# Strided attention before a dense layer: transposes by DMA instead of TensorE from batch 2 on

## The chip, the cores and the metric

One core of a Trainium2 chip runs the whole program. The metric is the device time of one execution in microseconds (us). Besides the unprofiled runs there is one profiled execution, from which all views of the trace come; its span goes from the first to the last instruction, and its own time is a little longer.

## The reference

Attention with two kinds of masks over 8 batches, 8 heads, 576 positions and 64 values a head, then a dense layer pair with a squared ReLU on the 4608 tokens:

```python
stride = 32
scores = (1 / sqrt(D)) * q @ k.T                     # per batch and head
rel = pos[:, None] - pos[None, :]
mask_local   = (rel >= 0) & (rel < stride)           # heads 0 to 3
mask_strided = (rel >= 0) & (pos[None, :] % stride == pos[:, None] % stride)   # heads 4 to 7
attn = softmax(where(mask, scores, -1e9))
x = (attn @ v).transpose(0, 2, 1, 3).reshape(4608, 512)
out = maximum(x @ w_in, 0) ** 2 @ w_out              # 512 -> 2048 -> 512
```

Inputs and output are float32; the kernel computes with bf16 operands.

## The kernel before, in words

**Units.** A unit `u` is one batch `b` and one pair of heads `p`; `u = 4*b + p`. Pairs 0 and 1 are local, pairs 2 and 3 strided. A local unit is cut into 6 blocks of 96 queries, a strided one into 8 groups of 72 positions (all positions with the same remainder by 8, which holds 4 residues by 32; the mask keeps the right one).

**Steps of a unit**, each emitted as one piece of the stream of TensorE:

- `step_T(u, "q")`, `step_T(u, "k")`: TensorE transposes q or k by blocks into one PSUM bank (L175; 8 matmuls for a strided unit, 6 for a local one), then ACT copies q (L188) and DVE copies k (L190) to SBUF as `qT`, `kT` (`kTl` for local units).
- `step_S(u)`: scores of both heads, one on each half of the array's rows (L214), into four PSUM banks; exponentials on ACT (L220) and masks on DVE (L226) are emitted one to four ticks later. A tick is one group of four dense matmuls.
- `step_D(u, part)`: attention times values, with a column of ones for the row sums (L251; two parts for a local unit, three for a strided one), a reciprocal and a product on DVE (L262, L263), into `x_l` or `x_s`.
- `step_E(u)`: TensorE transposes x (L274), and ACT (first three batches) or DVE (later) copies it into `xt[p]` (L280 local, L282 strided), where tokens are columns.

The PSUM pool `ps_t` of these steps has five banks, which are handed out in turn.

**Dense layers.** Nine chunks `c` of 512 tokens. `mm1(c, ff)` is a group of four matmuls into `ph` (L294) with a ReLU on ACT (L297) and a square on DVE one tick later (L298). `mm2(c, i)` is a quarter of a row block (L309); after the last quarter ACT copies `y` (L313) and SP stores it (L315).

**Order.** The steps of batch 0 run first. The list `groups` then holds all dense groups: chunk 0 and 1 one layer after the other, first layer of chunk 2 alone, and from chunk 3 on one group of `mm1(c)` alternating with one of `mm2(c-1)`. `stream_steps` lists the attention steps of batches 1 to 7, with T two units ahead of D, and `due` spreads them evenly between the groups, so that batch `b` is done before the first group of chunk `b` (batch 1 and 2 by groups 32 and 56). Everything is written out by hand: each engine runs its instructions in this order.

**Loads.** `loads(b)` is called at a given group (`load_at`: batch 2 at group 8, batch `b+2` two groups after batch `b` is done). It puts q, k and v of the local units and v of the strided ones on SP's queue as float32, with casts on POOL (L95, L123, L124, L139), and q and k of the strided units as casting DMAs on POOL's queue (L104), one unit after another between the casts. SP runs its issues in order, stores of `y` among them.

Of the kernel before, what the change touches and what calls it, by code (L numbers as in the profile page):

```python
# [9 lines left out]
BF16 = mybir.dt.bfloat16  # L10
# [4 lines left out]
def kernel(  # L15
# [9 lines left out]
    nc = tc.nc  # L25
    B, H, S, D = q.shape
    d_model, d_ff = moe_w_in.shape
    T = B * S
# [3 lines left out]
    QL = 96  # L32
    NL = S // QL
    NJ = 8
    RH = STRIDE // NJ
    SP_ = RH * NA
# [3 lines left out]
    singles = ctx.enter_context(tc.tile_pool(name="singles", bufs=1))  # L40
    qk_st = ctx.enter_context(tc.tile_pool(name="qk_st", bufs=2))
    qk_in = ctx.enter_context(tc.tile_pool(name="qk_in", bufs=3))
    qkT = ctx.enter_context(tc.tile_pool(name="qkT", bufs=3))
    v_st = ctx.enter_context(tc.tile_pool(name="v_st", bufs=2))
    small = ctx.enter_context(tc.tile_pool(name="small", bufs=4))
    x_pool = ctx.enter_context(tc.tile_pool(name="x_pool", bufs=2))
    g_pool = ctx.enter_context(tc.tile_pool(name="g_pool", bufs=2))
    r_pool = ctx.enter_context(tc.tile_pool(name="r_pool", bufs=4))
    y_pool = ctx.enter_context(tc.tile_pool(name="y_pool", bufs=3))

    PS = bass.MemoryType.PSUM
    ps_h = ctx.enter_context(tc.tile_pool(name="ps_h", bufs=2, space=PS))
    ps_y = ctx.enter_context(tc.tile_pool(name="ps_y", bufs=1, space=PS))
    ps_t = ctx.enter_context(tc.tile_pool(name="ps_t", bufs=5, space=PS))

# [11 lines left out]
    xt = [singles.tile([128, T], BF16, name=f"xt{p}") for p in range(4)]  # L67
# [6 lines left out]
    units = [(b, p) for b in range(B) for p in range(H // 2)]  # L74
    st = {}

    def is_local(u):
        return units[u][1] < H // 4

    def load_qk_local(u, eng, gate=None):  # L80
        b, p = units[u]
        s = st.setdefault(u, {})
        for name, src in (("q", q), ("k", k)):
            t = qk_st.tile([QL, 2, 6 * D], FP32, name=f"{name}_st")
            if gate is not None and name == "q":
                nc.gpsimd.tensor_copy(t[0:1, 0, 0:1], gate)
            eng.dma_start(out=t, in_=src[b, 2 * p:2 * p + 2]
                          .rearrange("h (p j) d -> p h (j d)", j=6))
            s[name + "f"] = t
# [9 lines left out]
    def load_qk_str(u):  # L99
        b, p = units[u]  # L100
        s = st.setdefault(u, {})
        for name, src in (("q", q), ("k", k)):
            t = qk_in.tile([SP_, 2, NJ * D], BF16, name=f"{name}_s")
            nc.gpsimd.dma_start(out=t, in_=src[b, 2 * p:2 * p + 2]  # L104
                                .rearrange("h (p j) d -> p h (j d)", j=NJ))
            s[name] = t

    def v_slot(u):
        b, p = units[u]
        return (b * 2 + p % 2) % NV  # L110

    def load_v_local(u, eng):
        b, p = units[u]
        t = vl_sts[p]
        for hh in range(2):
            eng.dma_start(out=t[32:128, NL * hh:NL * (hh + 1), :],
                          in_=v[b, 2 * p + hh].rearrange("(t p) d -> p t d", p=QL))
        st.setdefault(u, {})["vf"] = t
# [10 lines left out]
    def load_v_str(u, eng):  # L129
        b, p = units[u]  # L130
        t = v_st.tile([SP_, 2, NJ * D], FP32, name="v_st")
        eng.dma_start(out=t, in_=v[b, 2 * p:2 * p + 2]
                      .rearrange("h (p j) d -> p h (j d)", j=NJ))
        st.setdefault(u, {})["vf"] = t

    def cast_v_str(u, copy=None):
        s = st[u]
        t = vss[v_slot(u)]
        (copy or nc.gpsimd.tensor_copy)(t[:, :, 0:D], s["vf"].rearrange("p h (j d) -> p (h j) d", d=D))  # L139
        s["v"] = t  # L140
# [12 lines left out]
    def later(n, fn, key=None):  # L153
        pending.append((clock[0] + n, key, fn))
# [41 lines left out]
    def step_S(u):  # L196
        s = st[u]
        qT, kT = s["qT"], s["kT"]
        local = is_local(u)
        w, n = (QL, NL) if local else (SP_, NJ)  # L200
        kn = 128 if local else SP_
        hn = n // 2
        e = es[u % 4]
        s["e"] = e
        banks = [[None, None], [None, None]]
        for half in range(2):
            for row in range(2):
                banks[row][half] = ps_t.tile([128, 512], FP32, name="pt")
            for i in range(hn):
                t = half * hn + i  # L210
                klo = w * t
                for row in range(2):
                    rows = slice(64 * row, 64 * row + 64)
                    nc.tensor.matmul(banks[row][half][0:kn, w * i:w * (i + 1)],  # L214
                                     kT[rows, klo:klo + kn], qT[rows, w * t:w * (t + 1)],
                                     start=True, stop=True)

        def expo(row, half):
            lo = S * row + S // 2 * half
            nc.scalar.activation(e[0:kn, lo:lo + S // 2], banks[row][half][0:kn, 0:S // 2],  # L220
                                 AF.Exp, scale=scale)

        def masks(row):
            x = e[0:kn, S * row:S * (row + 1)].rearrange("p (t c) -> p t c", c=w)
            m = mask_loc if local else mask_str
            nc.vector.tensor_tensor(x, x, m.to_broadcast([kn, n, w]), op=ALU.mult)  # L226

        expo(0, 0)
        later(1, lambda: expo(0, 1), u)
        later(2, lambda: (masks(0), expo(1, 0)), u)  # L230
        later(3, lambda: expo(1, 1), u)
        later(4, lambda: masks(1), u)
# [33 lines left out]
    def step_E(u):  # L266
        s = st[u]
        b, p = units[u]
        x = s["x"]
        local = is_local(u)  # L270
        n, w = (NL, QL) if local else (NJ, SP_)
        px = ps_t.tile([128, S], BF16, name="pt")
        for t in range(n):
            nc.tensor.transpose(px[:, w * t:w * (t + 1)],  # L274
                                x[:, 2 * t:2 * t + 2, :].rearrange("p h d -> p (h d)"),
                                ident[0:w, 0:w])
        dst = xt[p][:, b * S:(b + 1) * S]
        copy = nc.scalar.copy if u < 12 else nc.vector.tensor_copy
        if local:
            copy(dst, px)  # L280
        else:
            copy(dst.rearrange("c (p j) -> c p j", j=NJ),  # L282
                                  px.rearrange("c (j p) -> c p j", j=NJ))
        st.pop(u)
# [43 lines left out]
    def first_steps():  # L328
# [9 lines left out]
        n = len(order)  # L338
        return [(fn, 0 if i < n - 8 else 4) for i, fn in enumerate(order)]

    def stream_steps(lo, hi, base):
        order = [T_(lo, "q"), T_(lo, "k"), T_(lo + 1, "q"), S_(lo), T_(lo + 1, "k")]
        ends = {}
        for u in range(lo, hi + 1):
            if u < hi - 1:
                order.append(S_(u + 1))
            if u > lo:
                order.append(E_(u - 1))
                ends[u - 1] = base + len(order)
            if u < hi:  # L350
                order.append(D_(u, 0))
                if u + 2 < hi:
                    order.append(T_(u + 2, "q"))
                order.append(D_(u, 1))
                if u + 2 < hi:
                    order.append(T_(u + 2, "k"))
                if not is_local(u):
                    order.append(D_(u, 2))
        return order, ends
# [5 lines left out]
    def loads(b):  # L365
        u = 4 * b
        for i in range(2):
            load_qk_local(u + i, nc.sync, gate=gates.get(b) if i == 0 else None)
            load_v_local(u + i, nc.sync)
        load_v_str(u + 2, nc.sync)  # L370
        load_v_str(u + 3, nc.sync)
        w_out = load_w_out if b == 1 else (lambda i: None)
        load_qk_str(u + 2)
        w_out(0)
        cast_qk_local(u, pool2)
        cast_v_local(u)
        load_qk_str(u + 3)
        w_out(1)
        cast_qk_local(u + 1, pool2)
        cast_v_local(u + 1)  # L380
        w_out(2)
        cast_v_str(u + 2)
        cast_v_str(u + 3)
        w_out(3)
# [92 lines left out]
    done_prev, g_prev = 0, 0  # L477
    ready = {1: 32, 2: 56}
    load_at = {8: 2}
    for b in range(1, B):  # L480
        g_end, s_end = ready.get(b, starts[b]), ends[4 * b + 3]
        if b == 1:
            g_prev = 9
        for g in range(g_prev, g_end + 1):
            due[g] = done_prev + (s_end - done_prev) * (g - g_prev) // (g_end - g_prev)
        done_prev, g_prev = s_end, g_end
        if b + 2 < B:
            load_at[g_end + 2] = b + 2
    done = 0
    for n, g in enumerate(groups):  # L490
        while done < due[n]:
            steps[done]()
            done += 1
        if n in load_at:
            loads(load_at[n])
        g()
        tick()
    for _ in range(4):
# [31 lines left out]
```

## Time and profile before

| what | value |
|---|---|
| median of 3 runs | 352.69 us (351.19 to 354.03) |
| the profiled execution's own time | 349.53 us |
| its span, first to last instruction | 347.8 us |
| granted clock of TensorE | 1.0 throughout |
| busy: PE, DVE, ACT, POOL | 315.1, 183.5, 177.3, 97.6 us |
| DMA | 37.67 MB |
| stores of y | 36, the first issued at 61.4 us |

In the views PE is TensorE's matmuls, PEld its weight loads, DVE VectorE, ACT ScalarE, POOL GpSimd and SP the engine that issues most DMAs (SPq, POOLq: their queues). A row of instructions gives the line of the kernel, the engine, the operation, what it writes and what it reads, shape and count, then busy time and mean duration of one in ns, then the idle time before and what ended it. Durations of matmuls overlap, so the time that one takes from the stream is read from the starts of neighbours in the timeline. In the timeline a row gives start and duration in us, and in brackets how long the engine was idle before it, and for whom.

### The profile page before, as it was taken

What the parts mean: (1) busy time and instruction counts of PE and PEld (TensorE: products, weight loads), DVE (VectorE), ACT (ScalarE), POOL (GpSimd) and SP (SyncE); (2) the same over time, 40 slices, a digit from 0 to 9 for tenths busy, and PEclk for the clock granted to TensorE, in tenths of its full rate; (3) what the DMA queues carried; (4) which work ended last, traced back from release to release, by engine and by line L of the source; (5) the groups of instructions that cost most, each with busy time, mean ns of one, the idle gap of its engine ahead of it and who ended that gap; (6) DMA issues with size and microseconds to landing.
All of it is one profiled execution on the core that took longest, in us unless ns stands there. A gap on an engine that the chain in (4) does not pass through costs nothing.

```text
span 347.8 us, 6912 instructions
## 1 busy us (share of the span) xinstructions
PE 315.1 (91%) x2752; PEld 166.6 (48%) x2752; DVE 183.5 (53%) x446; ACT 177.3 (51%) x356; POOL 97.6 (28%) x126
## 2 busy tenths in 40 slices
PE   2679769878899999999999999999999999999995
PEld 1575335444455554555555555454455444444442
DVE  5585563748665687656674666566446422222200
ACT  3746554567644675555555555554554344444411
POOL 6253852936404950700084007300000000000000
PEclk9999999999999999999999999999999999999999
DMA  7999999896209991330494039300000000100021
GB/s 179 214 174 232 192 178 232 216 242 114 36 32 230 254 201 24 67 64 30 117 238 79 34 94 225 80 30 32 32 30 32 30 31 32 61 30 32 30 90 61
DMA packets 44192, 37.67 MB, mean 108 GB/s; under 512 B 22400, under 2 KB 37248, under 8 KB 44160
## 3 DMA queue, kind: packets, MB, share of 16 engines
q1 hardware_dynamic: 33280, 28.32, 31.7%
q0 software_dynamic: 10880, 8.92, 17.5%
q8 instruction: 21, 0.34, 0.4%
q14 instruction: 11, 0.09, 0.1%
HBM read 36.70 MB, written 9.44 MB: 133 GB/s over the span
## 4 chain that ended last, share of the span: by engine, by line
PE 70%; DVE 12%; ACT 6%; DMA 6%; issue 2%; SPq 1%; POOL 1%; ACTq 0%; POOLq 0%
PE ph L294 27%; PE py L309 23%; PE ph L309 8%; DVE g_sb L298 4%; DMA vl_st<-in_v_dram 3%; PE pt L214 3%; ACT r L297 3%; PE pt L251 3%; PE pt L175 3%; DMA k_st<-in_k_dram 2%; PE pt L274 2%; DVE e L226 2%; DVE kTl L190 1%; DVE xt L282 1%; DVE x_s L263 1%
## 5 line engine op out<-in xcount | busy, mean ns | idle before, releaser
L294 PE MATMUL ph<-xt,w_in_b 128*128 128x512 bf16 x576 | 147.6, 379 | 1.1 <-DVE xt L282 1.0
L297 ACT ACTIVATE r<-ph 128x512 bf16<-128x512 f32 x144 | 86.1, 598 | 97.5 <-PE ph L294 96.1
L298 DVE TENSOR_TENSOR g_sb<-r 128x512 bf16<-128x512 bf16 x144 | 69.8, 486 | 113.3 <-ACT r L297 113.2
L309 PE MATMUL py<-w_out_b,g_sb 128*128 128x512 bf16 x400 | 102.8, 379 | 0.0
L309 PEld LDWEIGHTS <-g_sb 128*128 128x128 bf16 x576 | 51.1, 98 | 52.9 <-issue 2.4
L294 PEld LDWEIGHTS <-w_in_b 128*128 128x128 bf16 x576 | 50.1, 98 | 46.9 <-issue 0.2
L220 ACT ACTIVATE e<-pt 72x288 bf16<-72x288 f32 (+1 forms) x128 | 48.8, 407 | 16.9 <-PE pt L214 16.6
L309 PE MATMUL ph<-w_out_b,g_sb 128*128 128x512 bf16 x176 | 42.8, 379 | 0.0
L251 PEld LDWEIGHTS <-e 72*128 72x128 bf16 (+1 forms) x448 | 25.3, 102 | 20.8 <-DVE e L226 3.6
L95 POOL CAST q_l<-q_st 96x768 bf16<-96x768 f32 x14 | 11.9, 849 | 72.4 <-DMA q_st<-in_q_dram 68.8
L263 DVE TENSOR_TENSOR x_s<-pt,rinv 72x384 bf16<-72x384 f32 (+1 forms) x48 | 24.4, 509 | 1.6
L188 ACT COPY qT<-pt 128x576 bf16<-128x576 bf16 x32 | 20.4, 638 | 9.1 <-PE pt L175 8.1
L262 DVE RECIPROCAL rinv<-pt 96x6 f32<-96x6 f32 (+2 forms) x80 | 14.6, 183 | 11.8 <-PE pt L251 11.8
L123 POOL CAST vl<-vl_st 128x768 bf16<-128x768 f32 x16 | 14.7, 922 | 21.0 <-DMA vl_st<-in_v_dram 21.0
L226 DVE TENSOR_TENSOR e<-e,mask_str 72x576 bf16<-72x576 bf16 x32 | 17.8, 558 | 3.8 <-ACT e L220 3.7
L313 ACT COPY y<-py 128x512 f32<-128x512 f32 x25 | 14.7, 586 | 8.8 <-PE py L309 8.8
L263 DVE TENSOR_TENSOR x_l<-pt,rinv 96x384 bf16<-96x384 f32 x32 | 17.7, 553 | 1.1
L313 ACT COPY y<-ph 128x512 f32<-128x512 f32 x11 | 6.4, 586 | 20.9 <-PE ph L309 18.6
L251 PE MATMUL pt<-vs,e 72*128 72x65 bf16 x256 | 16.7, 200 | 0.4 <-DVE e L226 0.4
L139 POOL CAST vs<-v_st 72x1024 bf16<-72x1024 f32 x15 | 16.9, 1152 | 0.4
L226 DVE TENSOR_TENSOR e<-e,mask_loc 128x576 bf16<-128x576 bf16 x32 | 15.9, 498 | 1.8 <-ACT e L220 1.8
L251 PE MATMUL pt<-vl,e 128*128 128x65 bf16 x192 | 11.8, 199 | 3.8 <-DVE e L226 2.8
(54 smaller groups left out, 217.7 us busy)
## 6 DMA issues: line engine op xcount, KB each, us to landing
out_dram<-y SPq DMA_DIRECT2D x36, 256.0 KB
q_st<-in_q_dram SPq DMA_DIRECT2D x16, 288.0 KB
k_st<-in_k_dram SPq DMA_DIRECT2D x16, 288.0 KB
vl_st<-in_v_dram SPq DMA_DIRECT2D x32, 144.0 KB
v_st<-in_v_dram SPq DMA_DIRECT2D x16, 288.0 KB
q_s<-in_q_dram POOLq DMA_DIRECT2D x16, 144.0 KB, 5.9
k_s<-in_k_dram POOLq DMA_DIRECT2D x16, 144.0 KB, 6.6
w_in_b<-in_moe_w_in_dram POOLq DMA_DIRECT2D x4, 512.0 KB, 7.0
```

The costliest lines, as they stand in the source:

```text
L123: nc.gpsimd.tensor_copy(t[:, :, :, 0:D].rearrange("p h t d -> p (h t) d"), s["vf"])
L139: (copy or nc.gpsimd.tensor_copy)(t[:, :, 0:D], s["vf"].rearrange("p h (j d) -> p (h j) d", d=D))
L188: nc.scalar.copy(o, i)
L220: nc.scalar.activation(e[0:kn, lo:lo + S // 2], banks[row][half][0:kn, 0:S // 2], AF.Exp, scale=scale)
L226: nc.vector.tensor_tensor(x, x, m.to_broadcast([kn, n, w]), op=ALU.mult)
L251: nc.tensor.matmul(po[:, n - n0, :], e[0:kn, pos(n):pos(n) + 128], rhs[0:kn, src(n), 0:D + 1], start=True, stop=True)
L263: nc.vector.tensor_tensor(x, po[0:w, 0:m, 0:D], rinv[0:w, 0:m].to_broadcast([w, m, D]), op=ALU.mult)
L294: nc.tensor.matmul(ph, w_in_b[:, kk, 128 * ff:128 * (ff + 1)], xt[kk][:, 512 * c:512 * (c + 1)], start=(kk == 0), stop=(kk == 3))
L297: nc.scalar.activation(r, ph, AF.Relu)
L298: later(1, lambda: nc.vector.tensor_tensor(g[:, ff, :], r, r, op=ALU.mult))
L309: nc.tensor.matmul(py, g[:, ff, 128 * j:128 * (j + 1)], w_out_b[:, ff, :], start=(ff == 0), stop=(ff == 15))
L313: nc.scalar.copy(y, py)
```

## The change

From batch 2 on (`XB = 2`), three things are done by DMA:

- Strided q and k of a whole batch (four heads each) are cast to bf16 by one DMA each into DRAM scratch of 1152 rows of 128 values (`cast_str_dram`, on POOL's queue): one row holds two neighbouring positions, even then odd. Six groups after `loads(b)`, `transpose_str(b)` puts two transposing DMAs on SP's queue that bring them to SBUF as 128 x 1152: the row of a value is its parity and its place in the head, the column counts position pairs of the four heads.
- The strided `step_T` are left out for these batches, and `step_S` reads q and k of a group at every fourth column, for stationary and moving operand alike.
- `step_E` of a local unit becomes one transposing DMA on SP's queue, from `x_l` in SBUF into `xt[p]`, without TensorE, PSUM or copy.

Batches 0 and 1 stay as they were. Strided q and k of these have a pool of their own now (`qs_in`), and `y_pool` has four buffers for three.

```diff
+    qs_in = ctx.enter_context(tc.tile_pool(name="qs_in", bufs=2))
-    y_pool = ctx.enter_context(tc.tile_pool(name="y_pool", bufs=3))
+    y_pool = ctx.enter_context(tc.tile_pool(name="y_pool", bufs=4))
+    dram = ctx.enter_context(tc.tile_pool(name="dram", bufs=2, space=bass.MemoryType.DRAM))
+    strT = ctx.enter_context(tc.tile_pool(name="strT", bufs=2))
...
+    XB = 2
+    big = {}
+
+    def cast_str_dram(b):
+        for name, src in (("q", q), ("k", k)):
+            t = dram.tile([4 * S // 2, 2 * D], BF16, name=f"{name}_d")
+            nc.gpsimd.dma_start(
+                out=t.rearrange("(x y) c -> x (y c)", x=16),
+                in_=src[b, H // 2:H].rearrange("h (x y) d -> (h x) (y d)", x=4))
+            big[b, name] = t
+
+    def transpose_str(b):
+        for name in "qk":
+            o = strT.tile([128, 4 * S // 2], BF16, name=f"{name}T_s")
+            nc.sync.dma_start_transpose(out=o, in_=big.pop((b, name)))
+            for i in range(2):
+                st.setdefault(4 * b + 2 + i, {})[name + "T"] = o[:, S * i:S * (i + 1)]
...
-                    nc.tensor.matmul(banks[row][half][0:kn, w * i:w * (i + 1)],
-                                     kT[rows, klo:klo + kn], qT[rows, w * t:w * (t + 1)],
+                    if not local and units[u][0] >= XB:
+                        c0 = S // 2 * (t // 4) + t % 4
+                        cols = slice(c0, c0 + 4 * w - 3, 4)
+                        lhsT, rhs = kT[rows, cols], qT[rows, cols]
+                    else:
+                        lhsT, rhs = kT[rows, klo:klo + kn], qT[rows, w * t:w * (t + 1)]
+                    nc.tensor.matmul(banks[row][half][0:kn, w * i:w * (i + 1)], lhsT, rhs,
                                      start=True, stop=True)
...
+        if local and b >= XB:
+            nc.sync.dma_start_transpose(
+                out=xt[p][:, b * S:(b + 1) * S].rearrange("c (t q) -> c t q", q=QL),
+                in_=x.rearrange("p n d -> p (n d)"))
+            st.pop(u)
+            return
...
+    def has_T(u):
+        return is_local(u) or units[u][0] < XB
...
-                if u + 2 < hi:
+                if u + 2 < hi and has_T(u + 2):
                     order.append(T_(u + 2, "q"))
...
-        load_qk_str(u + 2)
+        if b >= XB:
+            cast_str_dram(b)
+        else:
+            load_qk_str(u + 2)
...
-        load_qk_str(u + 3)
+        if b < XB:
+            load_qk_str(u + 3)
...
+    tr_at = {}
...
         if n in load_at:
             loads(load_at[n])
+            tr_at[n + 6] = load_at[n]
+        if n in tr_at:
+            transpose_str(tr_at[n])
         g()
```

More of the change, by code (lines that the diff above doesn't have):

```diff
@@ L102, in load_qk_str @@
         for name, src in (("q", q), ("k", k)):
-            t = qk_in.tile([SP_, 2, NJ * D], BF16, name=f"{name}_s")
+            t = qs_in.tile([SP_, 2, NJ * D], BF16, name=f"{name}_s")
             nc.gpsimd.dma_start(out=t, in_=src[b, 2 * p:2 * p + 2]
@@ L351, in stream_steps @@
                 order.append(D_(u, 0))
-                if u + 2 < hi:
+                if u + 2 < hi and has_T(u + 2):
                     order.append(T_(u + 2, "q"))
                 order.append(D_(u, 1))
-                if u + 2 < hi:
+                if u + 2 < hi and has_T(u + 2):
                     order.append(T_(u + 2, "k"))
```

## The prediction

> **What bounds the kernel now.** I read the page first: the shares of busy time, the slices, the chain that ended last.
>
> ```profile
> span 347.8 us, 6912 instructions
> PE 315.1 (91%) x2752; PEld 166.6 (48%) x2752; DVE 183.5 (53%) x446; ACT 177.3 (51%) x356; POOL 97.6 (28%) x126
> PE   2679769878899999999999999999999999999995
> PEclk9999999999999999999999999999999999999999
> DMA  7999999896209991330494039300000000100021
> PE 70%; DVE 12%; ACT 6%; DMA 6%; issue 2%; SPq 1%; POOL 1%; ACTq 0%; POOLq 0%
> ```
>
> TensorE is busy 91% of the span, and from the twelfth slice (about 100 us) every slice but the last shows a 9; DVE and ACT stand near half. The DMA engines are full for some 80 us (slices of 8.7 us) and then only in bursts. So there are two stages. The table by stages, with us, then busy time of PE, PEld, DVE, ACT and POOL, says the same of the later ones:
>
> ```profile
> 135.00:275.00 140.00, 136.57 (x1249) 71.38 (x1248) 84.58 (x204) 74.37 (x153) 30.28 (x36) 1.00 0.32 74
> 275.00:347.00 72.00, 68.56 (x317) 30.91 (x316) 13.61 (x32) 26.14 (x44) 0.00 (x0) 1.00 0.12 46
> ```
>
> From 135 to 275 us, where attention of the later batches runs between matmuls of the two dense layers, TensorE is busy 136.57 of 140 us. After 275 us only dense matmuls are left, which the change doesn't touch. TensorE work taken out before 275 us should therefore come off the end nearly one for one, if nothing else comes late. What one piece of it is worth isn't the duration of an instruction, since matmuls overlap, but the distance to the next start:
>
> ```profile
> 182.81 0.42 PE L175 MATMUL pt<-ident,k_s 72*128 72x72 bf16 x8
> 183.07 1.03 PE L309 MATMUL py<-w_out_b,g_sb 128*128 128x512 bf16 x4
> 184.68 0.47 PE L214 MATMUL pt<-qT,kT 64*72 64x72 bf16 x16 [0.58 <-DVE kT L190]
> 185.08 1.04 PE L294 MATMUL ph<-xt,w_in_b 128*128 128x512 bf16 x4
> 185.96 0.42 PE L274 MATMUL pt<-ident,x_l 96*128 96x96 bf16 x6
> 186.21 1.03 PE L309 MATMUL py<-w_out_b,g_sb 128*128 128x512 bf16 x4
> ```
>
> Eight strided transposes hold the stream from 182.81 to 183.07: 0.26 us. Six local ones of x hold it from 185.96 to 186.21: 0.25 us. The sixteen strided score matmuls take 0.40 us (184.68 to 185.08), and before them TensorE stood idle 0.58 us for kT, the DVE copy of just such transposes.
>
> **The change part by part.**
>
> *Transposes removed.* Their counts over all 8 batches:
>
> ```profile
> L175 PE MATMUL pt<-ident,k_s 72*128 72x72 bf16 x128 | 7.3, 203 | 0.0
> L175 PE MATMUL pt<-ident,q_s 72*128 72x72 bf16 x128 | 7.3, 203 | 0.0
> L274 PE MATMUL pt<-ident,x_l 96*128 96x96 bf16 x96 | 7.2, 215 | 0.9 <-DVE x_l L263 0.9
> ```
>
> Six batches of eight lose theirs: 24 steps of eight (96 of 128 matmuls for k, as many for q) at 0.26 us are 6.2 us, and 12 steps of six (72 of 96) at 0.25 us are 3.0 us. Together **9.2 us of TensorE time**, all of it in the steps of batches 2 to 7, which end before 275 us, on the engine that sets the end. With them go 12 ACT copies of q, 12 DVE copies of k and 12 copies of local x; both engines have half their time free, so these are worth nothing directly.
>
> *Waits removed.* TensorE's waits between 69 and 275 us (total us, times, longest):
>
> ```profile
> PE pt L214 <- DVE kT L190: 4.8, 8, 1.4
> PE pt L214 <- DVE kTl L190: 2.5, 4, 1.1
> PE pt L251 <- DVE e L226: 1.5, 1, 1.5
> PE ph L294 <- DVE xt L282: 1.0, 5, 0.2
> PE pt L274 <- DVE x_s L263: 0.9, 2, 0.5
> ```
>
> The first row is the strided scores waiting for kT. With kT already brought by DMA these 4.8 us go. What is late next is the PSUM banks: a strided scores step takes four of five, and now that transposes no longer stand between, the third and fourth bank of the scores before are the first that it reuses, which exponentials free three ticks later. Four steps lie between; a batch now has 22 steps over 24 groups of dense matmuls (batch 2) or 32 (later), so that is 4.4 or 5.8 groups, and mostly the banks are free, not always. Ends: 4.8 us gained, or nothing if another wait takes each place. Nearest is the first row itself; I take 3.6 us, three quarters. The other rows stay: local transposes, strided x and its copy aren't touched.
>
> *Strided operands.* From batch 2 on the strided scores read q and k at every fourth element. No TensorE read in this trace has a step. The nearest rows are two pairs of copies, each first with a step of six or eight elements on its output, then without:
>
> ```profile
> L282 ACT COPY xt<-pt 128x576 bf16<-128x576 bf16 x6 | 3.7, 641 | 3.8 <-PE pt L274 3.8
> L280 ACT COPY xt<-pt 128x576 bf16<-128x576 bf16 x6 | 3.8, 638 | 4.5 <-PE pt L274 4.3
> L190 DVE COPY kTl<-pt 128x576 bf16<-128x576 bf16 x16 | 12.0, 750 | 1.1 <-PE pt L175 1.1
> L190 DVE COPY kT<-pt 128x576 bf16<-128x576 bf16 x16 | 7.2, 449 | 0.8 <-PE pt L175 0.7
> ```
>
> Ends: nothing, as on ACT (641 and 638 ns), or by DVE 750/449 = 1.67 times the 0.40 us, which over 12 units is 12 x 0.40 x 0.67 = 3.2 us. Reading faster than without a step is excluded, the columns being as many. I take nothing: both rows are writes of another engine, but ACT's shows that a step need not cost. The Trainium skill (SBUF — State Buffer, section Specifications (TRN2)) says that SBUF lines are 16 bytes and full rate needs two hits on a line; every fourth bf16 is 8 bytes, two to a line, so by it the sum keeps its nothing.
>
> *Casts and transposes on the queues.* Per batch POOL issues two casts of a whole batch's strided q and k instead of four of a unit each, and SP gets two transposes of 288 KB and two of 144 KB (local x) more; in all SP issues 24 DMAs more, POOL 12 fewer. SP and POOL around batch 2, and TensorE's need:
>
> ```profile
> 50.54 0.71 POOL L104 DMA_DIRECT2D q_s<-in_q_dram  x1 [0.33 <-PE pt L251]
> 51.24 0.69 POOL L104 DMA_DIRECT2D k_s<-in_k_dram  x1
> 58.05 1.26 SPq L132 DMA_DIRECT2D v_st<-in_v_dram  x2
> 61.40 7.31 SPq L315 DMA_DIRECT2D out_dram<-y  x4
> 68.79 0.38 SPq L87 DMA_DIRECT2D q_st<-in_q_dram  x1
> 72.20 0.82 POOL L95 CAST q_l<-q_st 96x768 bf16<-96x768 f32 x1 [1.94 <-DMA q_st<-in_q_dram]
> 83.29 0.47 PE L214 MATMUL pt<-qT,kT 64*72 64x72 bf16 x16 [0.39 <-DVE kT L190]
> 92.44 0.42 PE L175 MATMUL pt<-ident,q_l 96*128 96x96 bf16 x6
> DMA packets 9347, 7.03 MB, mean 220 GB/s; under 512 B 5372, under 2 KB 8429, under 8 KB 9343
> ```
>
> The transposes of batch 2 stand on SP behind that batch's loads (issued until 59.3 us) and wait for the casts, issued at 50.5 and 51.2 us into full DMA engines. Behind them on SP wait four output stores of chunk 0 and then, at 68.8 us, the loads of batch 3. The stores have four buffers now, so that ACT and TensorE can go on without them; batch 3's q is cast at 72.2 us and needed at 92.4 us, 19 us or so of cover. Batch 2's first strided scores run at 83.3 us. So the pair may take from 59 to about 83 us, 24 us, before anyone on TensorE feels it. In later batches the transposes are issued 24 of a batch's 32 groups ahead of its first steps, which is more. A local x transpose has the strided half of its batch as cover, about half of the distance from one dense chunk to the next:
>
> ```profile
> 205.39 0.38 PE L294 MATMUL ph<-xt,w_in_b 128*128 128x512 bf16 x1 [0.20 <-DVE xt L282]
> 241.02 0.38 PE L294 MATMUL ph<-xt,w_in_b 128*128 128x512 bf16 x1 [0.20 <-DVE xt L282]
> ```
>
> Chunk 5 to chunk 6 are 35.6 us, half is some 17 us. What a DMA transpose takes isn't in this trace. The nearest rows are the strided casting loads, from issue to landing (min, median, max):
>
> ```profile
> DMA to landing us min/median/max: 3.3/5.9/8.3
> DMA to landing us min/median/max: 3.4/6.6/9.0
> ```
>
> By bytes a 288 KB transpose is then 6.6 us (twice the fastest) to 18 us (twice the slowest), and a 144 KB one 3.3 to 9.0 us: all inside the covers of 24 and 17 us as single transfers, except two slow ones in a row (36 us). I take nothing, hidden work, and keep the price of lost cover for the rivals. POOL's casts are off the path, and POOL loses its waits for buffers of strided q and k.
>
> **Sum.** 9.2 + 3.6 = 12.8 us, against the profiled execution: span 347.8 to 335.0 us, its own time 349.5 to 336.7 us. That execution lies 3.2 us under the median 352.69 of the runs shown, so on the median's scale it is 352.69 - 12.8 = **340 us**.
>
> **The rivals.**
>
> *Waits come back, or the step costs.* If banks and DVE take the place of kT's wait wholly: 352.7 - 9.2 = 343.5 us. If the strided reads cost 3.2 us and the waits come back too: 346.7 us. For it: five PSUM buffers are tight. Against: ACT and DVE have half their time free and lose work.
>
> *The transposes run one after another and set the pace, level.* If those of a batch together take as long as the present 35.6 us from chunk to chunk, TensorE's gain is given back: about 352 us. In the Trainium skill (VectorE: DVE Perf Modes, section The three transpose paths) one 128x128 block by DMA is given as 1309 ns; a batch has 27 such blocks, which as an estimate is 35.3 us, this very case. Another page (Advanced Engine Details and Errata, section X-Bar Transpose (TRN2)) holds transposing DMAs as fast as plain ones, which would leave the forecast. No row here can choose between the two.
>
> *Slower than before.* The same mechanism past the point of 35.6 us per batch: at twice the median landing (13.2 us) for two strided and the median (6.6 us) for two local transposes a batch has 39.6 us of them in SP's one queue. Strided scores then wait for their q and k, and the loads behind wait as well; 4.0 us a batch over the five batches from the third on gives 352.7 + 20 = 373 us. For it: one queue, and DMA engines already a third busy (0.32 in the table of stages). Against: landings there are latency in large part and overlap, and 220 GB/s were moved between 48 and 80 us, at which 864 KB take 4 us.
>
> **How the numbers follow.** Forecast 340 us: 0.58. Waits back or steps costing, 343 to 347 us: 0.24. Level, 352 us: 0.09. Slower, 373 us: 0.09. Low end: both the 4.8 us and, with a lighter DVE, the 2.5 us for kTl go, 352.7 - 9.2 - 7.3 = 336.2, less the 1.5 us by which the lowest run lies under the median: 334.7. High end: 346.7, and 1.6 us more should the strided reads double (4.8 for 3.2 us), and 1.3 us of scatter upwards: 349.6. Runs of this kernel lie up to 0.4% from their median, so about 1% (3.5 us) is what can be told from no change. Faster by more: 0.82; within: 0.09; slower: 0.09.
>
> **What would show it.** TensorE's rows for strided q_s and k_s transposes should fall to 32 each and for x_l to 24; its wait on kT should be gone after 69 us, with no wait on a DMA in its place; sixteen strided scores should still be 0.40 us from the next start; distance between chunks about 33.5 us; everything after the last attention step unchanged at some 73 us. The prediction is wrong if TensorE waits for the transposed q, k or x, if SP's stores come so late that ACT waits for a buffer of y, or if strided scores stretch.

## The result, and the profile after

| | before | after |
|---|---|---|
| median | 351.94 us (4 runs, 350.88 to 354.03) | 339.72 us (4 runs, 336.85 to 343.57) |
| profiled execution: own time, span | 349.53, 347.8 us | 340.29, 338.5 us |
| ratio of the times | 1 | 0.9619, 95% interval 0.9532 to 0.9705 |

Medians, here and below, take all executions; ratios leave out slow ones, which show a lower granted clock (here the one of 343.57 us).

The kernel became 12.2 us faster by the medians; 340 us were forecast. The number is right, but the sum behind it is not: it leaves out a cost of 3.4 us, as the experiments show, so the closeness is in part luck. First the page of the kernel after, with the lines that answer to those of before: busy time, slices, chain.

```profile
PE 306.4 (91%) x2446; PEld 160.1 (47%) x2488; DVE 176.4 (52%) x424; ACT 167.4 (49%) x342; POOL 89.7 (27%) x114
PE   2579579997899998999999999999999999999995
DMA  7999999999845999670299329900410000100021
PE 78%; DVE 9%; DMA 5%; ACT 3%; issue 2%; POOL 1%; SPq 1%; ACTq 0%; POOLq 0%
```

TensorE is still the bound, and more so: its share of the chain went from 70% to 78%, DVE's from 12% to 9%. The groups by form show what left the stream:

```profile
L196 PE MATMUL pt<-ident,k_s 72*128 72x72 bf16 x32 | 2.2, 226 | 0.0
L306 PE MATMUL pt<-ident,x_l 96*128 96x96 bf16 x24 | 2.2, 243 | 0.9 <-DVE x_l L289 0.9
L196 PE MATMUL pt<-ident,q_s 72*128 72x72 bf16 x32 | 2.2, 225 | 0.0
```

32, 32 and 24 are left of 128, 128 and 96, those of batches 0 and 1. Of TensorE's waits from 69 us to the end of attention (total us, times, longest), these two changed most, beside the one that is gone:

```profile
PE ph L326 <- DVE xt L314: 2.6, 5, 1.6
PE pt L241 <- DVE kTl L211: 1.3, 3, 0.7
```

The wait for kT, 4.8 us before, is gone, and no DMA stands in its place. The wait for kTl fell from 2.5 to 1.3 us, and that for DVE's copy of strided x (`xt`) rose from 1.0 to 2.6 us. SP's queue around the transposes of batch 2, with start and duration of each issue:

```profile
60.73 3.17 SPq L125 DMA_TRANSPOSE qT_s<-q_d  x1
64.01 5.15 SPq L125 DMA_TRANSPOSE kT_s<-k_d  x1
69.25 2.39 SPq L347 DMA_DIRECT2D out_dram<-y  x4
71.74 0.57 SPq L90 DMA_DIRECT2D q_st<-in_q_dram  x1
...
88.44 2.56 SPq L299 DMA_TRANSPOSE xt<-x_l  x2
```

They go out right behind batch 2's loads, as forecast; the stores are issued 8 us later than before and the loads of batch 3 only 3 us (71.74 against 68.79). What the forecast did not have is in the strided scores:

```profile
137.02 0.75 PE L241 MATMUL pt<-qT_s,kT_s 64*72 64x72 bf16 x16
137.70 1.04 PE L341 MATMUL py<-w_out_b,g_sb 128*128 128x512 bf16 x4
```

Sixteen of them now hold the stream from 137.02 to 137.70: 0.68 us, for 0.40 us before.

**Where the time went, stage by stage.** The time to the end of chunk 0, which the change touches least, differs between the kernels of the table by 3.6 us (67.76 to 71.38), which goes in large part with the granted clock (rows below): e11, a changed kernel too, took 67.38 us there at 1.00. So stages are measured between fixed points: the fourth copy of `y` of a chunk on ACT, which ends it. Chunk 4 of the kernel before and after, for instance, is 239.95 - 204.32 and 233.16 - 199.38 us:

```profile
204.32 0.59 ACT L313 COPY y<-py 128x512 f32<-128x512 f32 x1 [0.43 <-PE py L309]
239.95 0.59 ACT L313 COPY y<-py 128x512 f32<-128x512 f32 x1 [0.43 <-PE py L309]
```

```profile
199.38 0.59 ACT L345 COPY y<-py 128x512 f32<-128x512 f32 x1 [0.43 <-PE py L341]
233.16 0.59 ACT L345 COPY y<-py 128x512 f32<-128x512 f32 x1 [0.43 <-PE py L341]
```

| stage (attention in it), us | before | after | no kT wait (e5) | contiguous (e10) |
|---|---|---|---|---|
| start to end of chunk 0 | 67.76 | 69.20 | 70.92 | 71.38 |
| chunks 1 and 2 (batches 2 to 4) | 101.12 | 96.40 | 101.35 | 93.60 |
| chunk 3 (batch 5) | 35.44 | 33.78 | 34.79 | 33.22 |
| chunk 4 (batch 6) | 35.63 | 33.78 | 34.79 | 33.22 |
| chunk 5 (batch 7) | 33.28 | 31.81 | 32.82 | 31.25 |
| to the last copy (none) | 70.41 | 69.74 | 70.42 | 69.73 |
| granted clock to the end of chunk 0 | 1.00 | 0.98 | 0.98 | 0.95 |
| granted clock in chunks 1 and 2 | 1.00 | 1.00 | 0.98 | 1.00 |
| granted clock in chunks 3 to 5 | 1.00 | 1.00 | 1.00 | 1.00 |

From the end of chunk 0 to the last copy the kernel after is 10.4 us faster (275.88 and 265.51 us); its profiled execution reached that point 1.4 us later, at a clock of 0.98 for 1.00. The 0.67 us of the last row stand in two rows of TensorE, the transposes of the last strided x, before and after:

```profile
273.03 0.36 PE L274 MATMUL pt<-ident,x_s 72*128 72x72 bf16 x6
273.90 0.24 PE L274 MATMUL pt<-ident,x_s 72*128 72x72 bf16 x2 [0.51 <-DVE x_s L263]
```

```profile
264.77 0.42 PE L306 MATMUL pt<-ident,x_s 72*128 72x72 bf16 x8
```

Before, they stopped for DVE's `x_s` after six of eight; after, with fewer steps to place, two dense groups stand between and all eight run through.

### The profile page after: what moved, and what is told of

Same layout as the page of the kernel before. It is cut to its first block, busy times and chain, and to the rows that moved or that the text cites. A ratio compares the mean times of both kernels' runs of the same rounds, so it can differ in the third digit from the quotient of the medians.

```text
span 338.5 us, 6368 instructions
## 1 busy us (share of the span) xinstructions
PE 306.4 (91%) x2446; PEld 160.1 (47%) x2488; DVE 176.4 (52%) x424; ACT 167.4 (49%) x342; POOL 89.7 (27%) x114
## 4 chain that ended last, share of the span: by engine, by line
PE 78%; DVE 9%; DMA 5%; ACT 3%; issue 2%; POOL 1%; SPq 1%; ACTq 0%; POOLq 0%
PE ph L326 30%; PE py L341 26%; PE ph L341 11%; PE pt L241 4%; PE pt L277 4%; DMA vl_st<-in_v_dram 3%; DVE g_sb L330 2%; PE pt L196 2%; DMA k_st<-in_k_dram 2%; DVE e L252 2%; PE pt L306 2%; ACT r L329 1%; DVE xt L314 1%; DVE x_s L289 1%; DVE kTl L211 1%
## 5 line engine op out<-in xcount | busy, mean ns | idle before, releaser
L326 PE MATMUL ph<-xt,w_in_b 128*128 128x512 bf16 x550 | 145.1, 381 | 4.1 <-DVE xt L314 2.6
L330 DVE TENSOR_TENSOR g_sb<-r 128x512 bf16<-128x512 bf16 x144 | 68.9, 480 | 113.0 <-ACT r L329 112.9
L341 PE MATMUL py<-w_out_b,g_sb 128*128 128x512 bf16 x390 | 100.8, 379 | 1.1 <-issue 0.8
L341 PEld LDWEIGHTS <-g_sb 128*128 128x128 bf16 x576 | 52.1, 98 | 58.1 <-issue 3.8
L326 PEld LDWEIGHTS <-w_in_b 128*128 128x128 bf16 x576 | 51.1, 98 | 50.4 <-issue 1.0
L246 ACT ACTIVATE e<-pt 72x288 bf16<-72x288 f32 (+1 forms) x128 | 48.0, 407 | 10.1 <-PE pt L241 10.0
L341 PE MATMUL ph<-w_out_b,g_sb 128*128 128x512 bf16 x170 | 41.5, 379 | 0.3
L252 DVE TENSOR_TENSOR e<-e,mask_str 72x576 bf16<-72x576 bf16 x32 | 19.4, 606 | 3.6 <-ACT e L246 3.3
L196 PE MATMUL pt<-ident,q_l 96*128 96x96 bf16 x96 | 7.4, 219 | 10.1 <-POOL mask_loc L447 5.2
L209 ACT COPY qT<-pt 128x576 bf16<-128x576 bf16 x20 | 12.7, 636 | 7.1 <-PE pt L196 6.9
```

What stands on the lines that cost most here:

```text
L326: nc.tensor.matmul(ph, w_in_b[:, kk, 128 * ff:128 * (ff + 1)], xt[kk][:, 512 * c:512 * (c + 1)], start=(kk == 0), stop=(kk == 3))
L330: later(1, lambda: nc.vector.tensor_tensor(g[:, ff, :], r, r, op=ALU.mult))
L341: nc.tensor.matmul(py, g[:, ff, 128 * j:128 * (j + 1)], w_out_b[:, ff, :], start=(ff == 0), stop=(ff == 15))
```

## The experiments

Theory A is the forecast's: TensorE's stream sets the pace from the second chunk on, so each edit is worth what it takes from or adds to that stream, plus waits. The rivals are named at each run. All compared times are ratios to the kernel before, run beside them on the same chip.

**e1, steps in the operands, alone.** Is it the step that makes the scores longer?

```diff
+    MODE = {2: (4, 1), 3: (1, 4), 4: (4, 4), 5: (2, 2), 6: (8, 8), 7: (3, 3)}   # batch: step of k, of q
...
+                        ks, qs = MODE[units[u][0]]
+                        cut = lambda s: slice(t % s, t % s + s * (w - 1) + 1, s) if s > 1 else slice(w * t, w * (t + 1))
+                        lhsT, rhs = kT[rows, cut(ks)], qT[rows, cut(qs)]
```

> The kernel before, transposes on TensorE kept, but the strided scores of each batch from 2 on read q and k at another step (other columns of the same tiles, so the scores are of other positions): batch 2 only the stationary operand k at step 4, batch 3 only the moving operand q at step 4, batch 4 both at step 4, batch 5 both at step 2, batch 6 both at step 8, batch 7 both at step 3. Read: distance from the first of the 16 score matmuls to the next group. Theory A (a step in the operand costs TensorE time): 0.40 us in batch 1, 0.68 us in batch 4 as in the changed kernel, more at step 8, batches 2 and 3 between 0.40 and 0.68. Rival B (the step is free, the changed kernel's 0.68 us come from tiles written by DMA or from tight PSUM banks): 0.40 us in all batches.

The timeline of TensorE, one strided scores step and the row behind it for batch 2 (only k at step 4), 3 (only q), 4 (both at 4), 5 (both at 2), 6 (both at 8) and 7 (both at 3):

```profile
90.60 0.74 PE L221 MATMUL pt<-qT,kT 64*72 64x72 bf16 x16 [1.29 <-DVE kT L190]
91.27 1.04 PE L300 MATMUL ph<-xt,w_in_b 128*128 128x512 bf16 x4
...
119.25 0.70 PE L221 MATMUL pt<-qT,kT 64*72 64x72 bf16 x16 [1.22 <-DVE kT L190]
119.89 0.82 PE L300 MATMUL ph<-xt,w_in_b 128*128 128x512 bf16 x3
...
143.14 0.75 PE L221 MATMUL pt<-qT,kT 64*72 64x72 bf16 x16
143.82 1.04 PE L315 MATMUL py<-w_out_b,g_sb 128*128 128x512 bf16 x4
...
178.96 0.47 PE L221 MATMUL pt<-qT,kT 64*72 64x72 bf16 x16
179.36 1.04 PE L315 MATMUL py<-w_out_b,g_sb 128*128 128x512 bf16 x4
...
214.41 1.33 PE L221 MATMUL pt<-qT,kT 64*72 64x72 bf16 x16
215.67 1.04 PE L315 MATMUL py<-w_out_b,g_sb 128*128 128x512 bf16 x4
...
253.30 0.61 PE L221 MATMUL pt<-qT,kT 64*72 64x72 bf16 x16 [0.39 <-DVE kT L190]
253.84 1.04 PE L300 MATMUL ph<-xt,w_in_b 128*128 128x512 bf16 x4
```

0.67, 0.64, 0.68, 0.40, 1.26 and 0.54 us; the second strided unit of each batch agrees to 0.01 us. Rival B falls: the step costs, without any DMA transpose in the kernel. Step 2 is free, step 4 costs 1.7 times, step 8 three times. One thing was not expected: either operand alone at step 4 costs nearly as much as both, as if the slower of the two reads set the time; making only q or only k contiguous would gain 0.04 us a step at most.

**e2 and e10, contiguous scores; e9, the changed kernel beside e10.** The order of rows in the scratch is changed, and the scores read without a step:

```diff
-                out=t.rearrange("(x y) c -> x (y c)", x=16),
-                in_=src[b, H // 2:H].rearrange("h (x y) d -> (h x) (y d)", x=4))
+                out=t.rearrange("(j r) c -> r j c", j=4),
+                in_=src[b, H // 2:H].rearrange("h (p j y) d -> (h p) j (y d)", j=4, y=2))
...
-                        c0 = S // 2 * (t // 4) + t % 4
-                        cols = slice(c0, c0 + 4 * w - 3, 4)
+                        c0 = 4 * w * (t % 4) + w * (2 * (u % 2) + t // 4)
+                        cols = slice(c0, c0 + w)
```

> The changed kernel with the rows of the DRAM scratch in another order: the cast writes them by position group, so that after the DMA transpose the 72 columns of a group lie side by side and the scores read without a step. Theory A: 16 scores take 0.40 us again, 12 x 0.28 = 3.4 us less than the changed kernel, about 336.5 us, ratio to before about 0.952; the cast now moves pieces of 512 bytes, which is hidden. Rival B: scores stay at 0.68 us, time of the changed kernel, ratio 0.962. Rival C (pieces of 512 bytes make the casts late): TensorE waits for q or k of batch 2, ratio above 0.962.

> The changed kernel once more, to stand beside the two below on one chip. Ratio to before 0.962 as measured at first; distance between chunks 33.8 us.

> The version with contiguous scores once more. If the 3.4 us that its scores save reach the end whole: 0.010 below the changed kernel beside it. If the casts in pieces of 512 bytes cost time in the first 110 us, where the loads fill the DMA engines: 0.005 (only the three later batches' 0.56 us each) or less.

e2 came to 339.03 us, ratio 0.9605 (0.9538 to 0.9672), which did not tell it from the changed kernel. Side by side with more runs the changed kernel (e9) took 339.86 us, ratio 0.9654 (0.9616 to 0.9692), and the contiguous one (e10) 335.66 us, ratio 0.9569 (0.9520 to 0.9619). In e10 the scores are back at 0.40 us:

```profile
143.01 0.47 PE L241 MATMUL pt<-qT_s,kT_s 64*72 64x72 bf16 x16
143.41 1.04 PE L341 MATMUL py<-w_out_b,g_sb 128*128 128x512 bf16 x4
```

and chunks 3, 4 and 5 each are 0.56 us shorter than in the changed kernel, twice 0.28 us to the hundredth. Theory A holds by these rows. The 0.0085 between e9 and e10 are 3.0 us, about the 3.4 us expected, though the two intervals touch.

**e11, step 2.** As e10, but pieces twice as long in the cast and scores at every second column:

```diff
-                out=t.rearrange("(j r) c -> r j c", j=4),
-                in_=src[b, H // 2:H].rearrange("h (p j y) d -> (h p) j (y d)", j=4, y=2))
+                out=t.rearrange("(j r z) c -> r j (z c)", j=2, z=2),
+                in_=src[b, H // 2:H].rearrange("h (p j y) d -> (h p) j (y d)", j=2, y=4))
```

> As the contiguous version, but the scratch holds two neighbouring rows side by side, so that the casts move pieces twice as long (1024 bytes read, 512 written) and the scores read at every second column. Step 2 cost nothing in the experiment on steps: 16 scores in 0.40 us. If longer pieces matter: faster than the contiguous version beside it, ratio about 0.952; if not, the same ratio as it.

335.52 us, ratio 0.9560 (0.9515 to 0.9605): the same as e10. The length of pieces makes no difference that shows here, and step 2 is free in place as well. These two versions beat both kernels.

**e3 and e4, one part of the change each.** e3 is the changed kernel with local x on TensorE again; e4 the kernel before with only local x by DMA.

```diff
-        if local and b >= XB:
+        if False and local and b >= XB:          # e3
```

```diff
+        if local and b >= 2:                     # e4
+            nc.sync.dma_start_transpose(
+                out=xt[p][:, b * S:(b + 1) * S].rearrange("c (t q) -> c t q", q=QL),
+                in_=x.rearrange("p n d -> p (n d)"))
```

> The changed kernel with local x transposed by TensorE again: only strided q and k go by DMA. Prediction's arithmetic: 12 steps x 0.25 us = 3.0 us more than the changed kernel, ratio to before 0.970. If local x by DMA were worth nothing (its wait moved to the DMA): ratio 0.962. If it were worth more than its matmuls: above 0.972.

> The kernel before with only local x transposed by DMA from batch 2 on: 12 x 0.25 = 3.0 us less than before by the prediction's arithmetic, ratio 0.9915. If gains add up, this and the strided part alone together give the whole change. Rival: the time that DVE and ACT save on the copies of local x shortens waits as well, ratio 0.985 or lower; or the transposes come late, ratio 1.0.

e3: 342.45 us, ratio 0.9691 (0.9608 to 0.9773), against 0.970 by arithmetic. Its chunks 3 and 4 show what local x alone is worth: from the fourth copy of one to that of the next they take 34.30 us,

```profile
172.80 0.58 ACT L345 COPY y<-py 128x512 f32<-128x512 f32 x1 [0.43 <-PE py L341]
207.10 0.58 ACT L345 COPY y<-py 128x512 f32<-128x512 f32 x1 [0.43 <-PE py L341]
```

0.52 us more than the 33.78 us of the changed kernel: two steps of 0.26 us a batch. e4: 348.01 us, ratio 0.9878 (0.9791 to 0.9965), between the arithmetic's 0.9915 and the rival's 0.985; its interval holds both, so the total alone is unclear. By chunks e4 gained 0.19, 0.45 and 0.52 us in 3 to 5 and 1.30 us in 1 and 2, together 2.5 us of the 3.0. Parts of 0.0309 and 0.0122 add up to 0.043, the whole was 0.038 and 0.035 (e9), so within their intervals they add.

**e5, the wait for kT, alone.** Transposes and copies stay, but the scores don't depend on kT:

```diff
+                    if not local and units[u][0] >= 2:
+                        lhsT = w_in_b[rows, 0, klo:klo + kn]
```

> The kernel before, all transposes on TensorE kept, but from batch 2 on the strided scores take a block of w_in, in SBUF since long, as stationary operand in place of kT (so these scores are not of the keys): the wait for kT is gone and nothing else. Theory A (the wait for kT was worth more than its 4.8 us of idle time, since stalls shorter than a pipeline's tail don't show as idle): from the fourth y copy to the last 5.2 us less than before (282.9 to 277.7 us), ratio about 0.985. The prediction's value: 3.6 us less. Rival B (PSUM banks or exponentials take the place): 0 to 2 us less.

350.57 us, ratio 0.9953 (0.9911 to 0.9995): 1.7 us, less than either value. By the table it gained 0.65, 0.84 and 0.46 us in chunks 3 to 5, where the kT wait was 1.7 us of idle time, and nothing that shows in chunks 1 and 2 (101.35 against 101.12 us). Two things stand against reading this as no gain, or as a gain. The stage varies: two profiles of one kernel at a clock of 1.00 differ by 2.5 us in it (e2 96.10, e10 93.60). And e5 ran there at a clock of 0.98, the kernel before at 1.00: it was 0.81 from 80 to 85 us and 0.85 from 85 to 90 us. Four matmuls of 512 columns then took 1.69 us (84.41 to 86.10), and 0.86 us soon after (89.23 to 90.09):

```profile
84.41 1.90 PE L297 MATMUL ph<-xt,w_in_b 128*128 128x512 bf16 x4
86.10 0.62 PE L175 MATMUL pt<-ident,k_s 72*128 72x72 bf16 x8
...
89.23 1.03 PE L297 MATMUL ph<-xt,w_in_b 128*128 128x512 bf16 x4
90.09 0.42 PE L175 MATMUL pt<-ident,q_s 72*128 72x72 bf16 x8
```

The two dense groups and two steps from 82.72 to 86.56 us took 3.84 us; at the distances from 89.05 to 90.35 us they would take 2.2 us. As an estimate that hides 1.7 us, and at a clock of 1.00 e5 would have gained some 1.5 us in chunks 1 and 2, 3.4 us in all. Whether the edit brought the lower clock isn't shown. TensorE's longest waits from 69 us on also say why a gain may be smaller there:

```profile
PE pt L217 <- DVE kTl L190: 2.1, 4, 0.8
PE pt L254 <- DVE e L229: 2.1, 1, 2.1
PE pt L217 <- DVE x_l L266: 1.4, 2, 0.9
```

In the last row the strided scores wait in their middle for DVE's `x_l`, which frees a PSUM bank. So in the later batches (32 groups a batch) the whole idle time came back, as theory A has it, though not its 5.2 us in all; for the early ones, where steps stand closer (24 groups), the row speaks for rival B in part and the estimate against it, and the size stays open.

**e6, every transpose three times.** How much room do the transposes have?

```diff
+            if b + 2 <= B:
+                for i in range(2):
+                    nc.sync.dma_start_transpose(out=xt[2 * i + "qk".index(name)][:, b * S:(b + 2) * S], in_=d)
```

(and the like for local x).

> The changed kernel with every DMA transpose of batches 2 to 6 issued three times, the copies into columns of xt that are not yet in use. Theory A (transposes are hidden; a batch's four cost 5.6 us of the DMA engines, by the shares of the traces of before and after 17.2 to 22.8 us of 33.8): 11.2 us more fill the engines to 34 of 33.8 us, so the time stays within 1% of the changed kernel, ratio 0.962 to 0.972, and the stores come later. Rival D of the prediction (transposes run one after another and set the pace near 35 us a batch): 70 us more a batch, far slower than before.

354.29 us, ratio 1.0039 (1.0001 to 1.0078): the whole gain is lost, which neither expected. The place matters. Chunks 3 and 4 took 33.78 us each, as without the copies, although the DMA engines' share was 1.09 in chunk 3, that is full (0.73 in chunk 4; chunk 5 has no copies). Lost were 14.0 us in chunks 1 and 2 (110.40 for 96.40 us). The timeline has 12.2 us of them in the two waits of TensorE, with the DVE and SP rows behind them:

```profile
112.25 0.49 PE L245 MATMUL pt<-qT_s,kT_s 64*72 64x72 bf16 x7 [4.79 <-DVE x_l L293]
144.19 1.44 PE L335 MATMUL ph<-xt,w_in_b 128*128 128x512 bf16 x3 [7.42 <-DMA xt<-x_l]
111.64 0.55 DVE L293 TENSOR_TENSOR x_l<-pt,rinv 96x384 bf16<-96x384 f32 x1 [6.33 <-DMA xt<-x_l]
103.48 3.28 SPq L303 DMA_TRANSPOSE xt<-x_l  x1
```

SP's queue reaches the first local x transpose of batch 2 only at 103.5 us, for 88.4 us in the changed kernel, since the twelve transposes of q and k ahead of it (six a batch, for batches 2 and 3) hold the queue for 1.3 to 3.4 us each while the DMA engines are full. `x_l` has two buffers, so the next batch's local units cannot write theirs (DVE, 6.33 us), the scores behind stop (4.79 us), and later the dense layer waits for x itself (7.42 us). The two copies behind each transpose of `x_l` read the same buffer, so a part of this is theirs. A lower clock adds to the loss: 0.67 from 110 to 115 us and 0.50 to 0.57 from 140 to 150 us, around these waits, where the changed kernel has 1.00 over the whole stage. The prediction's slower rival exists, then, in the early stage and through SP's order, not as a pace of 35 us a batch.

**e7, from batch 1 on.** The contiguous version with batch 1 by DMA too, its transposes of q and k issued at group 4:

```diff
-    XB = 2
+    XB = 1
...
-    tr_at = {}
+    tr_at = {4: 1}
```

> The version with contiguous scores, with everything from batch 1 on instead of batch 2. Theory A (TensorE's stream is the bound there too): four steps of 0.26 and two of 0.25 us less, 1.5 us, ratio 0.956 against 0.9605. Rival (the first 70 us are bound by the loads, into which batch 1's casts and transposes fall): batch 1's q and k come late, TensorE waits in batch 1, ratio 0.96 to 0.98.

349.82 us, ratio 0.9833 (0.9731 to 0.9936): 0.0228 above the contiguous version's 0.9605 (e2), some 8 us. The rival holds:

```profile
PE pt L241 <- DMA kT_s<-k_d: 11.7, 1, 11.7
```

Later TensorE waits once more, 4.9 us for local x by DMA. In the first 80 us the casts and transposes of one batch more were not hidden.

**e8, local q and k by DMA as well.** The contiguous version, with casts of local q and k into scratch rows of both heads:

```diff
+                t = dram.tile([S, 2 * D], BF16, name=f"{name}_dl{i}")
+                nc.gpsimd.dma_start(out=t.rearrange("s (h d) -> h s d", h=2),
+                                    in_=src[b, 2 * i:2 * i + 2])
```

> The version with contiguous scores, and local q and k from batch 2 on also cast to DRAM scratch (in pieces of 128 bytes) and brought in by DMA transposes; two small pools lose a buffer to make room. Theory A (TensorE's stream is the bound): 24 steps of 0.26 us, 6.2 us, and most of the waits for kTl go, together 7 to 9 us, about 331 us, ratio 0.938. Rival (small pieces fill the DMA engines, which are at 0.7 of a batch's time already): transposed q and k come late, TensorE waits for them, ratio 0.96 or more.

509.12 us, ratio 1.4469 (1.4364 to 1.4574). The rival holds, far beyond its number: TensorE is busy 63% of the span and waits 133 us for transposed local k; its granted clock, 1.0 before, was 0.82 in the mean, so the slowdown is not the waits alone. The software queue's line of the page, after it that of the contiguous version (e2), with packets, MB and share of 16 engines:

```profile
q0 software_dynamic: 241472, 13.23, 50.9%
```

```profile
q0 software_dynamic: 19904, 8.92, 21.4%
```

0.509 x 507.4 = 258 us of all DMA engines, against 0.214 x 338.1 = 72 us. That the 128-byte pieces make the difference is argued from packets twelve times as many; the longer POOL queue and the smaller pools were not tried apart.

## Why the prediction was right or wrong

- **Bound.** Right. In chunks 3 to 5 everything adds up in TensorE's stream: transposes -1.04 (four steps of 0.26), local x -0.50, scores +0.56, and the kT wait -0.65, -0.84, -0.46 as e5 has it: -1.63, -1.82, -1.44 us. Measured: -1.66, -1.85, -1.47.
- **Transposes, 9.2 us.** Right: the balance of chunks 3 to 5 closes with 0.26 us a step, and local x gave 0.52 us a batch (e3), which over six batches is 3.1 us for 3.0 forecast.
- **Strided operands, taken as nothing.** This step failed. It put ACT's row above DVE's; the cost was 1.70 times, 12 x 0.28 = 3.4 us. That this lies at DVE's end (1.67 times, 3.2 us) is luck, since the rows were misread: as the kernel writes these copies, their output goes through in order, and the step, of 96 or 72 elements, is on what they read from PSUM. Neither row said anything of TensorE's reads from SBUF. The rule drawn on beside it, two hits on a 16-byte line for full rate (the Trainium skill, SBUF — State Buffer, section Specifications (TRN2)), is not what e1 shows for TensorE: two elements to a line cost 1.7 times, four were free.
- **Waits, 3.6 us.** Right in kind, and 1.0 us larger in the pair of profiles: -10.4 us from the end of chunk 0, less -9.2 and +3.4, leaves 4.6 us, just inside the end of 4.8. Of these, 2.0 us are the wait for kT in chunks 3 to 5 (e5: 0.65 + 0.84 + 0.46) and 0.7 us the stall of the last strided x, which the forecast let stand. The rest is in chunks 1 and 2: their 4.7 us, less three batches of 1.54 us for transposes and local x and with 1.7 us for scores, leave 1.8 us. There the waits of TensorE add up to 8.2 us before and 6.1 us after. The largest, gone after, was

```profile
PE pt L214 <- DVE kT L190: 3.1, 5, 1.4
```

  and one for `xt` came in its place (0.2 to 1.6 us). The difference of 2.1 us is about these 1.8 us. How much of it is kT's own stays open (e5), and 1.0 us too much or too little is less than this stage varies between two profiled executions of one kernel (2.5 us).
- **The sum.** 12.8 us forecast, 10.4 us by the profile from the end of chunk 0, 12.2 us by the medians, and 10.8 to 13.5 us by the interval of e9. The total is right within what the runs can tell; the terms are not. In the pair of profiles 3.4 us too good and 1.0 us too bad cancel in part and leave 2.4 us; where the runs make these up isn't shown. That the medians lie only 0.6 us from the forecast is luck as much as working.
- **Transposes hidden.** Right, with a margin: one set is hidden; three are not in chunks 1 and 2 (e6). The DMA engines' shares of chunks 3 and 4 rose from 0.51 of 35.3 and 0.46 of 35.7 us to 0.70 and 0.65 of 33.8 us, so a batch costs them 22.8 - 17.2 = 5.6 us more (after, then before):

```profile
165.60:199.40 33.80, 33.01 (x281) 17.23 (x284) 20.82 (x48) 17.71 (x39) 10.12 (x12) 1.00 0.70 146
199.40:233.20 33.80, 33.01 (x282) 17.25 (x284) 21.27 (x48) 17.72 (x39) 9.73 (x10) 1.00 0.65 128
```

```profile
169.00:204.30 35.30, 34.52 (x326) 18.08 (x323) 22.37 (x52) 19.15 (x40) 11.88 (x14) 1.00 0.51 115
204.30:240.00 35.70, 34.73 (x332) 18.29 (x329) 22.25 (x52) 19.32 (x41) 10.13 (x12) 1.00 0.46 105
```

  Of the two pages of the Trainium skill that were weighed, neither fits. At 1309 ns a block one after another (the Trainium skill, VectorE: DVE Perf Modes, section The three transpose paths) the 27 blocks would take 35.3 us as an estimate, which no run shows. The other holds transposing DMAs as fast as plain ones (the Trainium skill, Advanced Engine Details and Errata, section X-Bar Transpose (TRN2)). The queue of loads, stores and transposes has, before and after, packets, MB and share of 16 engines:

```profile
q1 hardware_dynamic: 33280, 28.32, 31.7%
q1 hardware_dynamic: 54784, 33.63, 45.2%
```

  The transposes are the 5.31 MB more, and 0.452 x 338.5 - 0.317 x 347.8 = 42.7 us of all engines, 7.1 us a batch, in the whole execution: 124 GB/s, for 257 GB/s before, about half as fast. (The 5.6 us above are lower, in part because the casts on POOL's queue cost 0.9 us a batch less.) Their packets are smaller, 247 bytes for 851 in the mean; that this is the reason isn't shown.
- **Rivals.** "Waits come back, or the step costs" was half true, since the step did cost. "Level" and "slower" did not come; e6 shows one way to them.

## What to carry to other kernels

Where TensorE's stream is full, a transpose on it costs its distance to the next start (0.25 us for six or eight small ones), and moving it to the DMA engines returned that here, except in the first 80 us, which the loads fill: the same edit one batch earlier lost some 8 us. A layout that a DMA can choose freely should put the columns that a matmul reads side by side, or at most every second; here that was worth another 3 to 4 us (3.0 by the ratios, 4.2 by the medians). And a sum that comes out right is not yet a right sum: only the runs that took its terms apart showed the cost that it had left out. Before two stages are compared, their granted clocks belong beside them.

## What the runs showed of the hardware that was not expected

- TensorE with 64 x 72 bf16 operands: 16 matmuls in 0.40 us at step 1 and 2, 0.54 at step 3, 0.68 at step 4, 1.26 at step 8; at step 4, one of the two operands with the step is enough (0.64 and 0.67 us).
- Three times the transposes left the 33.78 us of chunk 3 unchanged with full DMA engines (share 1.09), and cost 14.0 us in chunks 1 and 2, where local x stood behind them in SP's queue.
- A transposing DMA of bf16 took about twice the engines' time of the other traffic on its queue: 124 GB/s against 257 GB/s.
